# A new order of all steps in a hand-scheduled kernel: windowed attention, then one expert per sentence

## The chip, the cores and the metric

The kernel runs on one core of a Trainium2 chip. The metric is the time of one execution on the device, in microseconds (us). A core has five engines that run their own instruction streams and wait for each other by semaphores: TensorE (PE; loading its weights is shown apart as PEld), VectorE (DVE), ScalarE (ACT), GpSimd (POOL) and SyncE (SP). [...] Sixteen DMA engines move data between HBM and SBUF; here nearly all transfers are issued on POOL's queue.

## The reference

For 8 sentences of 576 positions, with 8 heads of width 64, the reference computes attention in which each position sees itself and the 63 before it; the heads are put side by side to x, 576 x 512. The mean of x over the sentence picks one of 8 experts, and the whole sentence goes through that expert:

```python
scores = scale * np.matmul(q, k.transpose(0, 1, 3, 2))
mask = (rel >= 0) & (rel < window)            # window = 64
attn = softmax(np.where(mask, scores, -1e9))
x = np.matmul(attn, v)                        # heads joined: B, S, D = 8, 576, 512
...
logits = x.mean(axis=1) @ w_gate              # D x 8
e = argmax(logits); gate = softmax(logits)[e]
out[b] = gate * (relu(x[b] @ w1[e]) @ w2[e])  # w1: 512 x 1024, w2: 1024 x 512 per expert
```

Inputs and output are fp32; q, k, v and the weights are cast to 16 bits on their way in.

## The kernel before, in words

A *unit* is one piece of the attention: for each of the 8 sentences (batches, b) four units of two heads each, over the first 512 positions, and a fifth, the *tail*, with the last 64 positions of all heads. Units are numbered 0 to 39; 5b + i is unit i of batch b, and i = 4 is the tail. An expert of a batch is worked off in 18 *chunks*: c b.0 to c b.7 multiply x by an eighth of w1 each (line 457, 8 matmuls of 512 columns), c b.8 does the same for the tail (line 466, 64 small matmuls), c b.9 to c b.16 are half-sums of four groups of output rows (line 499), and c b.17 is the output's tail (line 508).

The program has no loops that set its order. A long string, OPS, lists every step by a letter and a number, and the kernel issues the steps in exactly that order, each on its engine's queue (lines 532 to 559). A step that is early in the list but on another engine runs beside the others; what orders two engines are the data and buffers alone. The letters:

- T: transposes of one unit's q and k by PE into PSUM (lines 226, 233); U: copy of the q part out of PSUM (243, 247); k: copy of the k part into kT (253, 256). Where U and k of one unit are on different engines they read the same PSUM tile, and the second waits for the first.
- S: scores by PE (276), with b also a matmul that adds the mask (270); E: exp by ScalarE (289, or 292 in two halves after an S with m); K: mask by a multiply on VectorE (298), for units without b.
- l: row sums by PE (310, 315); n and R: ln and exp(-ln) on ScalarE, the reciprocal (352, 358); A: attention times V by PE (332, 340); X: A's result times R, into x and its sum for the mean (VectorE, 365, 371).
- g, G, H, I: the gate of a batch: products and a sum on VectorE with a small PE matmul (380 to 388), the largest logit and its index (399 to 403), softmax sum on ScalarE (428), reciprocal (434). P reads the expert's number into a register of POOL (409); everything behind P on POOL's queue waits for it.
- Q, t, L, W: loads on POOL's queue: q and k of a batch (Q 2b and 2b+1, line 110), their tails (133), five V tiles (L 5b to 5b+4, lines 141 and 145), four weight halves of the chosen expert (W 4b to 4b+3, lines 419 and 422: w1's columns for chunks 0 to 3 and 4 to 7, w2's rows for the first and the second half-sums). V: two copies that shift V (150, 151). Y and C: loads on SP's queue and casts for a part of batch 0.
- c: the next chunk of the list of chunks. r: the evacuation of the next finished chunk from PSUM: relu and gate (442, 444) or a copy of output rows (478, 483). O and o: store of the next finished output rows, by POOL's queue or by SP's (488). r b.j and O b.j below name the chunk they belong to.
- i, x, y, m, M, z: constants: the identity, two bands, the masks, zeroes.

A letter a or d behind T, U, k, A, C or r picks ScalarE or VectorE for a copy; m takes the PSUM buffer from the pool `mo`, three banks that chunks use too, instead of the step's own single buffer. So a step that takes a `mo` buffer waits until the third buffer before it has been read out.

The chunk list is fixed; where a chunk stands between the other steps is set by the place of the c in OPS. Batch b's first chunk needs x of all its five units, the gate and W 4b. The list holds 885 steps.

Of the kernel before, what the change touches and what calls it, by code (L numbers as in the profile page):

```python
# [1 line left out]
OPS = (  # L2
# [35 lines left out]
).split()  # L38

# [17 lines left out]
def kernel(  # L57
# [11 lines left out]
    B, H, S, D = q.shape  # L69
# [88 lines left out]
    mb = const.tile([128, 4, 16], FP16)  # L158
# [215 lines left out]
                    accum_out=pool[b][:, 1, n:n + 1])  # L374

    gpss = {}

    def gate0(b):
        gpr = gpool.tile([128, 2, NP, E], FP32, tag="gpr", name="gpr")
        nc.vector.tensor_tensor(  # L380
            out=gpr, in0=pool[b].unsqueeze(3).broadcast_to([128, 2, NP, E]),
            in1=wg.unsqueeze(1).broadcast_to([128, 2, NP, E]), op=ALU.mult)
        grd = gpool.tile([128, E], FP32, tag="grd", name="grd")
        nc.vector.tensor_reduce(out=grd, in_=gpr.rearrange("p c n e -> p e (c n)"), op=ALU.add,
                                axis=mybir.AxisListType.X)
        gps = ps_a.tile([128, E], FP32, tag="lb", name="gps")
        for c in range(2):
            nc.tensor.matmul(out=gps[64 * c:64 * c + 64], lhsT=ones32[:, 0:64], rhs=grd,
                             start=True, stop=True, skip_group_check=True)
        gpss[b] = gps  # L390
# [122 lines left out]
    def chunks():  # L513
        for b in range(B):
            for ft in range(9):
                yield lambda b=b, ft=ft: w1_chunk(b, ft)
            for r in range(4):
# [6 lines left out]

    unit_ops = {"K": unit_k, "E": unit_e, "l": unit_l, "n": unit_n, "R": unit_r, "X": unit_x}
    unit_eops = {"T": unit_tp, "U": unit_q, "k": unit_kt, "S": unit_s, "A": unit_a}
    batch_ops = {"g": gate0, "G": gate1, "H": gate_w, "I": gate2, "V": shift_v,
                 "P": pick, "W": load_w, "L": load_v, "t": load_tail}
    setup_ops = {"i": make_ident, "x": lambda: band(mb, 1), "y": lambda: band(mt, 0),
                 "m": main_mask, "M": tail_mask, "z": zero_v}  # L530

    with tc.manual_schedule():
        for op in OPS:
            c, x = op[0], op[1:].lstrip("abdm")
# [55 lines left out]
```

## Time and profile before

| what | us |
|---|---|
| median of 3 runs | 206.81 (206.77 to 208.1) |
| the profiled execution, its own time | 206.57 |
| span of its instructions in the profile | 205.0 |
| PE busy | 185.3 |
| ScalarE (ACT) busy | 133.6 |
| VectorE (DVE) busy | 119.5 |
| POOL busy, mostly issuing transfers | 110.0 |

The profile covers one execution. Its rows are read as follows. A timeline row has the start in us from the span's first instruction, the duration, the engine, the line, the operation, output <- inputs, and in square brackets the engine's idle time just before it and what ended that. A group row has the instructions of one kind with their count, then busy us and mean ns of one, then idle us before them. A row of the stage view has for each engine its busy us in that stretch and the number of instructions, then the granted PE clock as a share of full speed, the DMA share and GB/s. In the page's rows of digits each digit is a fortieth of the span, in tenths. Matmul ends are modelled, so a pipelined matmul looks longer than the pace at which matmuls follow each other. A transfer's row is its issue alone; the row "DMA to landing" tells the time from there to its arrival.

### The profile page before, as it was taken

What the parts mean: (1) busy time and instruction counts of PE and PEld (TensorE: products, weight loads), DVE (VectorE), ACT (ScalarE), POOL (GpSimd) and SP (SyncE); (2) the same over time, 40 slices, a digit from 0 to 9 for tenths busy, and PEclk for the clock granted to TensorE, in tenths of its full rate; (3) what the DMA queues carried; (4) which work ended last, traced back from release to release, by engine and by line L of the source; (5) the groups of instructions that cost most, each with busy time, mean ns of one, the idle gap of its engine ahead of it and who ended that gap; (6) DMA issues with size and microseconds to landing.
All of it is one profiled execution on the core that took longest, in us unless ns stands there. A gap on an engine that the chain in (4) does not pass through costs nothing.

```text
span 205.0 us, 8089 instructions
## 1 busy us (share of the span) xinstructions
PE 185.3 (90%) x3513; PEld 123.7 (60%) x3518; DVE 119.5 (58%) x343; ACT 133.6 (65%) x252; POOL 110.0 (54%) x157
## 2 busy tenths in 40 slices
PE   0549785999999999899999999999999999999991
PEld 0436563866685755657666676777566565655651
DVE  2055967786458695688588749566566258211041
ACT  3169998955588757879975992795577634525600
POOL 7968927514943384438824633436935622852650
PEclk9996999699999999999999999999999999999998
DMA  6999999999999999999999999999999999799995
GB/s 137 174 184 154 186 164 199 206 203 123 149 194 195 188 182 193 186 197 159 183 195 194 201 202 188 191 298 183 167 245 210 198 163 332 198 201 176 404 339 189
DMA packets 83538, 41.16 MB, mean 201 GB/s; under 512 B 48080, under 2 KB 80976, under 8 KB 83504
## 3 DMA queue, kind: packets, MB, share of 16 engines
q0 software_dynamic: 81696, 38.94, 137.0%
q1 hardware_dynamic: 1200, 1.64, 2.3%
q8 instruction: 27, 0.44, 0.8%
q10 hardware_dynamic: 608, 0.08, 0.3%
q14 instruction: 7, 0.06, 0.1%
HBM read 61.88 MB, written 9.44 MB: 348 GB/s over the span
## 4 chain that ended last, share of the span: by engine, by line
PE 74%; ACT 10%; DVE 8%; issue 3%; DMA 3%; POOL 0%; DVEq 0%; POOLq 0%
PE po L499 26%; PE ph L457 24%; PE tp L226 5%; PE ph L466 4%; PE s L276 4%; PE av L332 3%; DMA km<-in_k_dram 3%; PE po L508 3%; ACT pe L289 2%; PE lb L310 2%; ACT ln L352 2%; DVE kT L253 2%; ACT rl L358 2%; ACT pe L292 1%; DVE qt L243 1%
## 5 line engine op out<-in xcount | busy, mean ns | idle before, releaser
L457 PE MATMUL ph<-xm,w1b 128*64 128x512 f16 x512 | 60.8, 379 | 0.4 <-ACT kT L253 0.4
L499 PE MATMUL po<-w2b,hm 128*64 128x512 f16 x512 | 59.7, 379 | 0.0
L499 PEld LDWEIGHTS <-hm 128*64 128x64 f16 x512 | 29.1, 110 | 21.1
L457 PEld LDWEIGHTS <-w1b 128*64 128x64 f16 x512 | 30.1, 110 | 19.3 <-issue 0.7
L141 POOL DMA_DIRECT2D vw<-in_v_dram x32 | 28.9, 909 | 19.2 <-DMA w1b<-in_moe_w_dram 4.4
L442 ACT ACTIVATE hm<-ph,gw 128x512 f16<-128x512 f32 x40 | 27.5, 691 | 13.6 <-PE ph L457 13.3
L365 DVE CUSTOM_DVE_ANT_0 xm<-av,rl 128x512 f16<-128x512 f32 x32 | 21.8, 687 | 13.0 <-PE av L332 9.8
L352 ACT ACTIVATE ln<-lb 128x512 f32<-128x512 f32 (+1 forms) x40 | 22.6, 565 | 8.9 <-PE lb L310 7.3
L358 ACT ACTIVATE rl<-ln 128x512 f32<-128x512 f32 (+1 forms) x40 | 23.2, 593 | 3.6 <-DVE pool L365 3.4
L478 DVE COPY ob<-po 128x512 f32<-128x512 f32 x16 | 11.1, 691 | 24.8 <-PE po L499 24.8
L488 POOL DMA_DIRECT2D out_dram<-ob x28 | 15.5, 560 | 14.9 <-DMA w2b<-in_moe_w_dram 7.6
L444 DVE TENSOR_SCALAR hm<-ph,gw 128x512 f16<-128x512 f32 x24 | 18.0, 748 | 7.9 <-PE ph L457 7.6
L289 ACT ACTIVATE pe<-s 128x1024 f16<-128x1024 f32 x19 | 19.7, 1038 | 1.3 <-PE av L332 0.9
L298 DVE TENSOR_TENSOR pe<-pe,mask 128x1024 f16<-128x1024 f16 x26 | 17.7, 685 | 4.7 <-ACT pe L289 3.9
L226 PE MATMUL tp<-ident,qm 128*64 128x128 bf16 x256 | 14.6, 241 | 6.5 <-ACT qm L128 4.7
L276 PEld LDWEIGHTS <-kT 64*128 64x128 bf16 x576 | 10.8, 97 | 11.5 <-issue 7.7
L478 ACT COPY ob<-po 128x512 f32<-128x512 f32 x16 | 9.4, 590 | 12.1 <-PE po L499 12.1
L253 ACT COPY kT<-tp 128x512 bf16<-128x512 bf16 x16 | 9.5, 608 | 10.7 <-DVE qt L243 5.8
L226 PEld LDWEIGHTS <-qm 128*64 128x64 bf16 x256 | 10.9, 123 | 9.2 <-ACT qm L128 4.7
L422 POOL DMA_DIRECT2D w2b<-in_moe_w_dram x16 | 12.7, 798 | 6.9 <-DMA w1b<-in_moe_w_dram 2.1
L276 PE MATMUL s<-qt,kT 64*128 64x64 bf16 x512 | 12.7, 195 | 3.9 <-ACT kT L253 2.5
L419 POOL DMA_DIRECT2D w1b<-in_moe_w_dram x16 | 12.6, 792 | 6.6 <-PE ph L457 3.3
(82 smaller groups left out, 274.2 us busy)
## 6 DMA issues: line engine op xcount, KB each, us to landing
w1b<-in_moe_w_dram POOLq DMA_DIRECT2D x16, 512.0 KB, 8.5
w2b<-in_moe_w_dram POOLq DMA_DIRECT2D x16, 512.0 KB, 12.8
out_dram<-ob POOLq DMA_DIRECT2D x28, 256.0 KB, 8.6
vw<-in_v_dram POOLq DMA_DIRECT2D x32, 128.0 KB, 9.2
qm<-in_q_dram POOLq DMA_DIRECT2D x7, 512.0 KB, 9.9
km<-in_k_dram POOLq DMA_DIRECT2D x7, 512.0 KB, 9.4
out_dram<-ob SPq DMA_DIRECT2D x4, 256.0 KB, 3.9
out_dram<-obt POOLq DMA_DIRECT2D x14, 64.0 KB, 5.4
```

The lines of the kernel that those rows point to most:

```text
L141: nc.gpsimd.dma_start(out=vt[:, 2 * J + 1], in_=v[b, :, 128 * J:128 * J + 128].rearrange("h c d -> c h d"))
L226: nc.tensor.transpose(tp[p0:p0 + 64, n, r], t[:, 2 * i + hh, ts(r, 64)], ident)
L276: nc.tensor.matmul(out=sp[hh][:, ts(m, 64)], lhsT=kq, rhs=qt[p0:p0 + 64, m], start=not pm, stop=True, skip_group_check=True)
L289: nc.scalar.activation(out=po, in_=sp[0], func=AF.Exp, scale=scale)
L352: nc.scalar.activation(out=ln, in_=lb[:, 0:n], func=AF.Ln)
L358: nc.scalar.activation(out=rl, in_=lns.pop((b, i)), func=AF.Exp, scale=-1.0)
L365: nc.vector.tensor_tensor_reduce(out=xm[:, i], in0=av.rearrange("q r p -> q (r p)"), in1=rl, scale=1.0, scalar=0.0, op0=ALU.mult, op1=ALU.add,
L442: nc.scalar.activation(out=o, in_=i, func=AF.Relu, scale=g)
L444: nc.vector.tensor_scalar(out=o, in0=i, scalar1=g, scalar2=0.0, op0=ALU.mult, op1=ALU.max)
L457: nc.tensor.matmul(out=ph[64 * c:64 * c + 64], lhsT=w1t[:, kb, ts(2 * ft + c, 64)], rhs=xm[:, kb], start=(kb == 0), stop=(kb == 3), skip_g ...
L478: copy(e)(out=ob, in_=po)
L499: nc.tensor.matmul(out=po[64 * c:64 * c + 64], lhsT=hm[:, fb, ts(2 * r + c, 64)], rhs=w2t[:, fb], start=(fb == 0), stop=(fb == 7), skip_gr ...
```

## The change

The list OPS is replaced by another order of the same work, 891 steps. It was searched on a replay of the program in which two copies out of one PSUM tile take turns, and in which lengths are scattered in six cases. In it

- some copies and casts are on another engine: 9 instead of 13 q copies and 20 instead of 21 k copies on ScalarE, both casts of batch 0 on VectorE;
- nine instead of seven units are masked by a matmul (b), so 31 instead of 33 by a multiply; 16 instead of 14 value units and 16 instead of 15 score units use `mo` buffers;
- 38 instead of 35 stores go by POOL's queue, 2 instead of 5 by SP's; of the last batch's, O7.10, O7.14 and O7.16 go by POOL's, o7.12 and o7.17 by SP's;
- the gate's small PE matmul is a step of its own, j, somewhere behind g.

The first and the last lines of both lists and the code:

```diff
--- before
+++ after
@@ -1,40 +1,40 @@
 OPS = (
-    "Y0.24 Y1.24 Q0.48 Q1.48 i Ca0.24 Cd1.24 T1 Tm3 x ka3 Q0.2 Q1.2 Tm2 Tm0 Ud3 Ua1 mb Sb3 "
-    "ka1 kd2 z Ua2 E3 Ua0 Q2 ka0 Q3 Sm2 S0 l3 E2 t0 E0 n3 Smb1 E1 Tm5 T4 K0 y L2 kd5 Tm8 L3 "
-    "ka4 Tm7 Mb Ua4 l1 K2 ka8 Sb4 R3 L4 Ud5 T6 n1 l2 kd7 Ud8 E4 L1 R1 Sb5 n2 l4 L0 Ud6 t1 ka6 "
-    "n4 R4 V0 Am3 l0 A1 L7 E5 Ud7 n0 T9 X3 Am2 kd9 R2 X1 Sb7 X2 R0 Q4 E7 A0 Q5 Ud9 l5 L5 Am4 "
-    "Smb6 X4 n5 Sb8 L6 E6 X0 L8 R5 l7 Sm9 T12 n7 E9 g0 Tm10 Ud12 G0 Ud10 E8 L9 Tm11 ka12 ka11 "
-    "S12 Tm13 H0 l6 Ud11 R7 V1 ka10 n6 kd13 t2 A5 Q6 X5 T14 E12 Ud13 A7 K9 Q7 X7 P0 l8 kd14 "
-    "W0 Am6 R6 S10 n8 l9 W1 Ud14 K12 E10 A8 Sm14 n9 S11 E14 X6 E11 Tm15 l12 Tm17 T16 K14 R8 "
-    "K10 Ud17 X8 Ud15 Tm18 n12 kd17 S13 W3 I0 A9 l10 ka15 K11 Ud18 c W2 ka18 t3 n10 c c R9 "
-    "l14 L11 rd E13 X9 c S17 L10 rd ra L13 n14 g1 G1 rd P1 c ra c R14 rd c c c ra L14 K13 ra "
-    "c c c H1 Ua16 ra l11 R12 c rd L12 W5 ra n11 c ka16 c l13 c ra V2 W4 Q9 A12 Q8 I1 c X12 "
-    "Am14 A10 R10 c rd X14 rd E17 T19 n13 S15 R11 X10 K17 ka19 Sm18 E18 c R13 Am11 l17 c Ud19 "
...
-    "ra l38 V7 c n38 ra R36 c c c ra W27 c O E39 O K39 c rd A35 O c X35 c l39 Am36 A38 rd R38 "
-    "I6 X36 ra c n39 O c rd Am39 O R39 O ra l37 c X38 X39 c rd A37 c c rd n37 c R37 ra X37 g7 "
-    "rd c ra ra G7 H7 c rd c O O O O P7 W28 c c ra W29 c ra W30 W31 O O O O O O O O O O O c c "
-    "ra O c rd O I7 c c c ra O c ra O c rd ra c c c ra ra ra c c c ra ra c ra c c ra c c rd o "
-    "rd o c c c c rd o rd o c ra o "
+    "Y0.24 Q0.48 Q1.48 Q0.2 x Cd0.24 y i Q1.2 Y1.24 Q3 Cd1.24 z Tm3 Tm2 mb T0 Tm1 ka3 ka2 ka0 "
+    "t0 Ud3 Ud2 Q2 Sb3 L0 L3 ka1 L1 L2 E3 Smb2 L4 Ud0 l3 Ud1 t1 S0 T4 E2 kd4 Ud4 n3 Smb1 E0 "
+    "Mb K0 E1 R3 Q4 L9 Tm5 Sb4 Tm7 Tm8 Ud5 Q5 ka5 kd8 E4 L5 kd7 l1 n1 T6 l4 n4 Ud7 l2 Sb5 ka6 "
+    "n2 R1 R4 l0 V0 A3 Ud6 L7 Am1 n0 E5 T9 X3 Am2 Ud9 S7 R2 L8 E7 Ud8 X1 R0 l5 X2 L6 n5 Smb6 "
+    "A0 Am4 K7 ka9 E6 t2 X4 X0 Sb8 l7 g0 n7 T12 j0 Q6 Sm9 Tm10 G0 Ud12 kd12 E8 Ud10 H0 E9 "
+    "Tm13 Tm11 R7 K9 l6 R5 ka10 Sb12 Ud11 ka13 V1 n6 Q7 l8 P0 Ud13 W0 I0 kd11 T14 Am5 A7 X7 "
+    "A6 Ud14 kd14 L12 n8 X5 E12 R6 l12 n12 Sm14 X6 S11 l9 E14 Smb10 Tm17 E11 n9 T18 W1 Ud17 "
+    "A9 W2 E10 S13 kd18 Ud18 L13 Tm15 Ud15 l10 Am8 R8 W3 kd15 ka17 T16 K14 L11 c X8 L14 n10 "
+    "E13 R9 c ra X9 c R10 c rd c g1 K11 rd S17 j1 G1 ra ra c H1 L10 c rd l14 K13 c t3 ra c P1 "
+    "n14 Q8 ra c c rd c V2 Ua16 c c ra ka16 l11 A10 X10 Am12 W4 c Q9 R12 X12 n11 ra W5 R11 "
+    "A11 rd W6 T19 E17 c l13 n13 R13 Ua19 I1 X11 c Sm18 S15 K17 L15 rd E18 W7 R14 A13 c l17 "
+    "ra X13 A14 c L16 L17 X14 g2 n17 Tm20 E15 ra kd19 c Ud20 ra L18 kd20 T22 S19 Sm16 E19 L19 "
...
+    "Ud38 A33 ra ka38 Am34 l35 T39 X33 c n35 W22 c ra X34 A31 X31 g6 kd39 c O Sm38 R35 O S37 "
+    "ra E38 j6 c c G6 P6 Ud39 E37 ra ra c V7 K38 rd H6 c l36 c K37 W24 n36 S39 A35 l37 ra rd "
+    "E39 c ra n37 c X35 R36 c A37 c ra l38 Am36 K39 ra c c O R37 rd X37 n38 Am39 X36 O c rd c "
+    "I6 l39 W27 R38 c n39 O O A38 rd R39 c W25 W26 ra X39 X38 g7 c j7 O c G7 c ra c P7 rd ra "
+    "c c O W29 O c ra c O rd H7 O ra c O c W28 W31 ra O ra O c ra c c ra rd c c c c rd c W30 "
+    "I7 O ra O c rd c c ra rd O c O O rd c O rd O O c rd c c O ra c c rd c O rd ra rd c c O "
+    "rd O c c ra O O c c c c ra rd o O c ra O c ra o "
 ).split()
@@ -374,6 +374,7 @@
                     accum_out=pool[b][:, 1, n:n + 1])
 
     gpss = {}
+    grds = {}
 
     def gate0(b):
         gpr = gpool.tile([128, 2, NP, E], FP32, tag="gpr", name="gpr")
@@ -383,6 +384,10 @@
         grd = gpool.tile([128, E], FP32, tag="grd", name="grd")
         nc.vector.tensor_reduce(out=grd, in_=gpr.rearrange("p c n e -> p e (c n)"), op=ALU.add,
                                 axis=mybir.AxisListType.X)
+        grds[b] = grd
+
+    def gate_mm(b):
+        grd = grds.pop(b)
         gps = ps_a.tile([128, E], FP32, tag="lb", name="gps")
         for c in range(2):
             nc.tensor.matmul(out=gps[64 * c:64 * c + 64], lhsT=ones32[:, 0:64], rhs=grd,
@@ -524,7 +529,7 @@
 
     unit_ops = {"K": unit_k, "E": unit_e, "l": unit_l, "n": unit_n, "R": unit_r, "X": unit_x}
     unit_eops = {"T": unit_tp, "U": unit_q, "k": unit_kt, "S": unit_s, "A": unit_a}
-    batch_ops = {"g": gate0, "G": gate1, "H": gate_w, "I": gate2, "V": shift_v,
+    batch_ops = {"g": gate0, "j": gate_mm, "G": gate1, "H": gate_w, "I": gate2, "V": shift_v,
                  "P": pick, "W": load_w, "L": load_v, "t": load_tail}
     setup_ops = {"i": make_ident, "x": lambda: band(mb, 1), "y": lambda: band(mt, 0),
                  "m": main_mask, "M": tail_mask, "z": zero_v}
```

35 rows, old and new, of the table OPS are left out of this document.

## The prediction

> **What bounds the kernel now.** I read the page first, then busy time by stage, then the chain of waits, then the row-by-row timeline where the stages meet.
>
> ```profile
> span 205.0 us, 8089 instructions
> PE 185.3 (90%) x3513; PEld 123.7 (60%) x3518; DVE 119.5 (58%) x343; ACT 133.6 (65%) x252; POOL 110.0 (54%) x157
> PE   0549785999999999899999999999999999999991
> PEclk9996999699999999999999999999999999999998
> DMA  6999999999999999999999999999999999799995
> ```
>
> PE has holes in the first eight slices and hardly any later. The DMA engines are full from the second slice on. The stage view says the same in us; its cuts are the start of the first expert chunk c0.0 (42.70), c2.0, c3.0 and the last matmul.
>
> ```profile
> core 0: us, PE busy (x) PEld busy (x) DVE busy (x) ACT busy (x) POOL busy (x), PEclk, DMA share, GB/s
> 12.40:42.70 30.30, 23.54 (x613) 17.71 (x617) 21.37 (x65) 27.51 (x52) 19.28 (x24) 0.89 1.72 184
> 42.70:83.60 40.90, 40.70 (x770) 27.90 (x771) 26.91 (x76) 28.87 (x56) 21.05 (x26) 1.00 1.56 178
> 83.60:107.50 23.90, 23.02 (x482) 15.22 (x478) 18.35 (x55) 20.14 (x38) 12.95 (x17) 1.00 1.62 183
> 107.50:200.80 93.30, 93.22 (x1598) 59.38 (x1592) 49.29 (x138) 53.20 (x102) 45.80 (x71) 1.00 1.26 228
> ```
>
> Before 42.70 ScalarE (ACT) is the busiest: 27.5 of 30.3 us. From 42.70 PE works without a break. What must PE still do there? The chain gives the pace when nothing waits:
>
> ```profile
> 112.59 0.34 PE s L276 x16
> ...
> 131.23 0.45 PE tp L226 x16
> ...
> 167.29 0.51 PE av L332 x32
> ...
> 185.06 6.91 PE ph L457 x64
> 191.96 1.01 PE ph L466 x64
> 192.97 6.91 PE po L499 x64
> 199.88 0.89 PE po L508 x16
> ```
>
> The last four rows are one batch's expert: 15.7 us, eight times 125.8. After c0.0 stand also 21 units' transposes (16 at 0.45, five tails at half: 8.3), 25 score units (7.5, at 0.34 and tails less), 28 row sums (two 512-column matmuls each, as the quarter of a chunk 0.22, tails half: 5.5), 30 value units (0.25, tails half: 6.8) and seven gates' tiny matmuls (taken as 1.0). Together 154.9. It ran from 42.70 to 200.8, 158.1: only 3.2 are lost after c0.0. So the time is: start of c0.0, plus 154.9 of PE work, plus a few us of stalls, plus 4.2 from the last matmul to the end of the span, plus 1.57 between the span (205.0) and the execution's own 206.57. The runs shown have a median of 206.81, 0.24 above it.
>
> **The change, step by step.** Counting the steps of both lists on each side of c0.0: PE's work behind c0.0 is the same set of steps, only reordered, so 154.9 stays. What can move is c0.0, the stalls and the tail.
>
> (1) *When ScalarE is ready for c0.0.* c0.0 waited here:
>
> ```profile
> 41.61 0.42 DVE L243 COPY qt<-tp 128x512 bf16<-128x512 bf16 x1
> 42.06 0.59 ACT L253 COPY kT<-tp 128x512 bf16<-128x512 bf16 x1 [1.09 <-DVE qt L243]
> 42.70 1.27 PE L457 MATMUL ph<-xm,w1b 128*64 128x512 f16 x10 [0.38 <-ACT kT L253]
> ```
>
> The middle row is ka15. It reads the tile that Ud15 has just read (copies out of one tile take turns); c0.0 takes ka15's PSUM buffer. ScalarE's work from the first exp (13.16) to there groups as follows:
>
> ```profile
> L289 ACT ACTIVATE pe<-s 128x1024 f16<-128x1024 f32 x8 | 8.3, 1041 | 1.1 <-PE av L332 0.7 <-PE s L276 0.4
> L253 ACT COPY kT<-tp 128x512 bf16<-128x512 bf16 x7 | 4.2, 632 | 1.3 <-DVE qt L243 1.1 <-PE tp L226 0.2
> L292 ACT ACTIVATE pe<-s 128x512 f16<-128x512 f32 x6 | 3.4, 629 | 0.0
> L243 ACT COPY qt<-tp 128x512 bf16<-128x512 bf16 x1 | 0.6, 580 | 0.0
> L247 ACT COPY qtt<-tpt 128x256 bf16<-128x256 bf16 x1 | 0.4, 378 | 0.0
> ```
>
> The new list has the same exp, ln and reciprocal steps there, but 5 kT copies for 7 (-1.26), no qt and no qtt copy (-0.96), and E10 in two halves (2 x 0.63 - 1.04 = +0.22): -2.0, and about 0.3 back because neighbouring rows overlap by 0.1: -1.7. The 1.09 before ka15 goes too: the buffer of c0.0 is now Tm17's, freed by ka17, whose partner Ud17 stands five steps ahead of the last VectorE step before c0.0. So ScalarE could be through at 42.65 - 1.7 - 1.1 = 39.9. The first exp starts as before: four transposes back to back now end at 11.8, where the mask made Sb3 start before. VectorE takes over four qt copies, a cast and a kT copy (about 2.7 us) and gives up three mask multiplies and X8 (2.8): even, and it was busy 21.4 of 30.3. PE makes two more masks by matmul (about 0.43 each, 0.9): hidden in its 6.8 idle us; without that cover +0.9.
>
> (2) *When the loads are there.* Q7 (K of batch 3) and W0 (first weight half):
>
> ```profile
> L110 POOL DMA_DIRECT2D km<-in_k_dram x1: 881/881/881, 28.7 to 28.7; - x1
> DMA to landing us min/median/max: 9.0/9.0/9.0
> ...
> L419 POOL DMA_DIRECT2D w1b<-in_moe_w_dram x1: 752/752/752, 32.0 to 32.0; - x1
> DMA to landing us min/median/max: 8.3/8.3/8.3
> ```
>
> Q7 landed at 37.7, W0 at 40.3: one full queue, 2.6 us per 512 KB, emptied in order. Both lists put the same loads ahead of W0, so W0 stays at 40.3 even if the gate comes earlier. Behind Q7 PE has four transposes (1.8), a value unit's tail, a score unit, a row sum and a value unit (0.9) before c0.0: 37.7 + 2.7 = 40.4. So c0.0 lies between 40.4 and 43.6 (nothing won, and the masks uncovered). Before, the same 2.7 us of work took 5.0. I take 41.0, near the low end since ScalarE's 39.9 lies below it: **-1.7**.
>
> (3) *Weights behind it.* V tiles now stand between the weight halves: W1 lands one V tile later (0.64 by size), near 43.5, and c0.4 is due at 41.0 + 4 x 0.86 = 44.4. W3 lands two later, near 49.2; c0.10 is due near 50.4. Hidden, with about a microsecond to spare; c0.0 beyond that can't pull the rest along.
>
> (4) *P1 on POOL's queue.* P1 reads the expert number of batch 1, and all loads behind it wait:
>
> ```profile
> 48.63 0.69 POOL L145 DMA_DIRECT2D vw<-in_v_dram  x1 [6.75 <-DVE hm L444]
> ...
> 49.00:53.00 4.00, 4.00 (x95) 3.05 (x92) 1.35 (x2) 3.09 (x8) 3.89 (x6) 1.00 1.36 89
> 53.00:57.00 4.00, 4.00 (x42) 2.67 (x39) 2.31 (x4) 1.84 (x4) 3.92 (x5) 1.00 1.18 176
> ```
>
> POOL stood 6.75 us, the queue ran dry, and 4 us passed at 89 GB/s instead of 176: 2 us of loads lost. The new list has two more V loads ahead of P1 (11.3 us of queue behind W0 for 10.3, by size) and G1 about a microsecond earlier, so this hole should close. PE did not wait for it, so I book 0 and keep 2 us of margin: loads then come early enough for a PE that is 1.7 us early.
>
> (5) *Stalls behind c0.0.* c2.0 to c3.0 took 23.9 for 22.4 of work, the largest loss, 1.5, with ScalarE at 84%. The new list spreads ScalarE's copies (in that stage 20.2 us by mean durations instead of 24.4) but gives VectorE 21.4 instead of 19.2. The gates' matmuls (new step j) no longer stand right behind their sums. From -1.5 to +3; I take **-0.4**.
>
> (6) *Tail.* Output O7.16 goes by POOL's queue, o7.17 by SP's as before:
>
> ```profile
> L488 POOL DMA_DIRECT2D out_dram<-ob x2: 540/540/540, 195.4 to 195.9; - x2
> DMA to landing us min/median/max: 4.5/4.6/4.6
> ...
> L488 SPq DMA_DIRECT2D out_dram<-ob x1: 332/332/332, 200.6 to 200.6; - x1
> DMA to landing us min/median/max: 2.7/2.7/2.7
> ```
>
> POOL's queue was still full there; the new list stores more before, and O7.16 is ready 0.9 us ahead of o7.17. Between 0 and +1; I take **+0.2**.
>
> Sum: 206.57 - 1.7 - 0.4 + 0.2 = **204.7**.
>
> **The rivals.**
> *A: c0.0 does not come early.* The clock row has two slices at 6: PE at half clock. A transpose unit then takes twice as long:
>
> ```profile
> 38.81 0.64 PE L226 MATMUL tp<-ident,qm 128*64 128x128 bf16 x8
> ...
> 39.67 0.50 PE L310 MATMUL lb<-pe,ones 128*64 128x512 f16 x2
> 40.00 0.39 PE L226 MATMUL tp<-ident,qm 128*64 128x128 bf16 x8
> ...
> 40.45 0.39 PE L226 MATMUL tp<-ident,qm 128*64 128x128 bf16 x8
> ```
>
> From 38.81 to 39.67 is one unit, 0.86; from 40.00 to 40.45 the next, 0.45. In the new list the 2.7 us behind Q7 set c0.0; at half clock throughout they take 5.4, c0.0 comes at 43.1, and the time is 206.6 + 0.4 - 0.2 = 206.8. For it: in the page each halved slice follows one in which PE was only 4 or 5 tenths busy, and PE will have holes before Q7 again. Against it: from about 40 on the clock was full. [...]
>
> *B: slower.* An engine falls behind PE in the middle. By mean durations ScalarE has 0.95, 0.91 and 0.92 of PE's time between c1.0, c2.0, c3.0 and c4.0, VectorE 0.97 in the second. If each of these three stages loses the 1.5 us of the worst stage of before, in waits for PSUM buffers, and the rest loses its 1.7, that is 6.2 for 3.2, +3; with c0.0 halfway (-0.8) and a full tail (+1), 209.8. From 1.5 us of stalls more than before, the main case's gain is gone. Against it: in the worst stage ScalarE's figure was 1.09.
>
> *C: more than expected.* c0.0 at 40.4, all of the 1.5 us gone, no tail: 206.57 - 2.3 - 1.5 = 202.8. For it: P1's hole closes. Against it: every hand-off must fit.
>
> **How the numbers follow.** Main case 0.45, itself 203.7 to 205.7; A 0.2; B 0.2; C 0.15. About 1% (2.1 us) is what a measurement of this kernel can tell from no change, so faster means below 204.7: C and a good half of the main case, 0.42. Slower means above 208.9: three quarters of B, 0.15. Within: 0.43. The range 202.6 to 208.9 leaves out that part of B and a third of C, 0.2 in all.
>
> **What would show it.** Right: c0.0 starts near 41.0, PE has nearly no idle time behind it, no 89 GB/s stretch near 50, and POOL's wait at P1 is covered. Wrong: c0.0 after 42, with ka17 or Q7 named (step 1 or 2); PE waits for W1 or W3 in batch 0 (3); idle PE between 60 and 125 behind VectorE or ScalarE (5); over 4.5 us from last matmul to end (6).

## The result, and the profile after

| | before | after |
|---|---|---|
| median of 20 runs each, us | 207.66 (206.56 to 209.9) | 205.5 (204.76 to 208.15) |
| ratio of the times, 95% interval | | 0.9932 (0.9905 to 0.996) |
| the profiled execution, its own time, us | 206.57 | 204.83 |
| span, us | 205.0 | 203.2 |

The change makes the kernel 0.7% faster; the interval reaches from 0.4% to 0.95%. The ratios here and below leave out runs more than 1.5% above the fastest of the same kernel. The profiled pair differs by 1.74; both lie at the fast end of their kernel's runs. The page of after, the rows that answer to those of before:

```profile
span 203.2 us, 8111 instructions
...
PE 184.5 (91%) x3522; PEld 124.4 (61%) x3522; DVE 120.1 (59%) x347; ACT 132.0 (65%) x247; POOL 112.4 (55%) x160
...
PE   0496786799999999999999999999999999999991
...
PEclk9999999999999999999999999999999999999997
```

PE still has its holes in the first eight slices, but in this execution none of them is followed by half clock, which before had two slices of (16 to 19 and 36 to 40 us). The clock row does not show the beginning: in the first 11 us the transposes of both kernels follow each other at half pace, a group of 8 every 0.43 us instead of 0.22. The stage view of after, cut at c0.0, c2.0, c3.0 and the last matmul (PE, PEld, DVE, ACT, POOL busy, then clock, DMA share, GB/s):

```profile
12.40:42.15 29.75, 23.23 (x622) 16.13 (x623) 20.70 (x61) 25.79 (x49) 18.94 (x24) 1.00 1.76 179
42.15:82.76 40.61, 40.61 (x792) 26.70 (x788) 26.29 (x76) 30.23 (x59) 21.75 (x27) 1.00 1.57 192
82.76:105.45 22.69, 22.69 (x470) 15.28 (x464) 19.20 (x57) 17.85 (x34) 14.14 (x18) 1.00 1.69 186
105.45:198.95 93.50, 93.42 (x1596) 62.79 (x1592) 49.33 (x136) 54.15 (x102) 46.10 (x72) 1.00 1.25 230
```

Two things are to be seen. Behind c0.0 PE waits for next to nothing, and the worst stage of before (c2.0 to c3.0, 23.90) takes 22.69. And c0.0 is hardly earlier, 42.15 for 42.70, although ScalarE's work ahead of it fell from 27.51 to 25.79. Where did that go? Rows of PE tell it (start, duration; in brackets the idle time before and what ended it):

```profile
17.80 0.41 PE L226 MATMUL tp<-ident,qm 128*64 128x128 bf16 x8 [1.55 <-DMA qm<-in_q_dram]
...
41.92 0.39 PE L226 MATMUL tp<-ident,km 128*64 128x128 bf16 x8
42.15 0.38 PE L462 MATMUL ph<-xm,w1b 128*64 128x512 f16 x2
```

c0.0 (line 462 here; the lines behind the new step j are five further down) waits for nothing itself. But ahead of 17.80 PE stands 1.55 us until Q2, the q of batch 1, has landed, and begins Tm5 0.05 behind it; before, Q2 and Q3 had landed by 15.76 and PE came to Tm5 at 17.29. The chain of waits, followed back from c0.0, runs through PE, ScalarE and VectorE to Tm5, from there to Q2 without another load, and on through POOL's issues to steps that POOL computes itself. Pieces of it, in order of time:

```profile
5.35 0.47 POOL ident L178
5.82 1.58 POOL km L110 x2
...
8.74 9.02 DMA qm<-in_q_dram
17.80 0.64 PE tp L226 x16
```

The loads are late from the start of the queue on. The view of busy time in 5 us windows, first after, then before:

```profile
5.00:10.00 5.00, 2.18 (x38) 1.94 (x40) 1.99 (x8) 0.59 (x2) 5.00 (x8) 1.00 1.25 152
10.00:15.00 5.00, 4.83 (x88) 2.96 (x86) 1.46 (x4) 3.55 (x6) 4.12 (x6) 1.00 1.41 149
```

```profile
5.00:10.00 5.00, 2.82 (x48) 2.14 (x46) 0.28 (x1) 0.53 (x2) 4.93 (x8) 1.00 1.37 173
10.00:15.00 5.00, 2.44 (x55) 1.69 (x52) 2.97 (x8) 3.46 (x7) 3.39 (x5) 1.00 1.55 186
```

The queue moved 152 and 149 GB/s instead of 173 and 186. The timeline of POOL in after shows what it did instead:

```profile
3.89 0.28 POOL L183 TENSOR_SCALAR_AFFINE_SELECT mb<-mb 128x64 f16<-128x64 f16 x1
...
5.31 0.51 POOL L178 TENSOR_SCALAR_AFFINE_SELECT ident<-ident 128x128 bf16<-128x128 bf16 x1
5.77 1.63 POOL L110 DMA_DIRECT2D km<-in_k_dram  x2
...
8.74 0.93 POOL L110 DMA_DIRECT2D qm<-in_q_dram  x1
```

From 3.89 to 5.8 POOL itself computes the two bands and the identity (x, y, i, five steps). Only then does it issue Q1.2 and Q3, in the row of 5.77, and Q2 comes at 8.74 where before issued it at 5.44.

### The profile page after: what moved, and what is told of

Same layout as the page of the kernel before. It is cut to its first block, busy times and chain, and to the rows that moved or that the text cites. A ratio compares the mean times of both kernels' runs of the same rounds, so it can differ in the third digit from the quotient of the medians.

```text
span 203.2 us, 8111 instructions
## 1 busy us (share of the span) xinstructions
PE 184.5 (91%) x3522; PEld 124.4 (61%) x3522; DVE 120.1 (59%) x347; ACT 132.0 (65%) x247; POOL 112.4 (55%) x160
## 4 chain that ended last, share of the span: by engine, by line
PE 66%; DMA 13%; POOL 6%; issue 6%; ACT 4%; DVE 2%; POOLq 1%; ACTq 0%; DVEq 0%
PE ph L462 21%; PE po L504 20%; PE tp L226 6%; DMA w2b<-in_moe_w_dram 4%; DMA w1b<-in_moe_w_dram 4%; DMA qm<-in_q_dram 4%; PE s L276 4%; PE av L332 3%; PE lb L310 3%; PE ph L471 3%; POOL out_dram L493 3%; PE po L513 2%; ACT ln L352 2%; POOL km L110 1%; ACT pe L289 1%
## 5 line engine op out<-in xcount | busy, mean ns | idle before, releaser
L462 PEld LDWEIGHTS <-w1b 128*64 128x64 f16 x512 | 31.8, 110 | 18.7 <-issue 0.4
L504 PEld LDWEIGHTS <-hm 128*64 128x64 f16 x512 | 30.1, 110 | 19.3
L447 ACT ACTIVATE hm<-ph,gw 128x512 f16<-128x512 f32 x39 | 26.6, 694 | 13.5 <-PE ph L462 13.3
L493 POOL DMA_DIRECT2D out_dram<-ob x31 | 17.2, 557 | 24.7 <-DMA w1b<-in_moe_w_dram 7.5
L483 ACT COPY ob<-po 128x512 f32<-128x512 f32 x18 | 10.6, 587 | 23.5 <-PE po L504 20.7
L449 DVE TENSOR_SCALAR hm<-ph,gw 128x512 f16<-128x512 f32 x25 | 18.7, 749 | 12.1 <-PE ph L462 11.6
L298 DVE TENSOR_TENSOR pe<-pe,mask 128x1024 f16<-128x1024 f16 x24 | 16.3, 686 | 4.0 <-ACT pe L289 3.3
L253 ACT COPY kT<-tp 128x512 bf16<-128x512 bf16 x19 | 11.2, 594 | 9.8 <-PE tp L226 8.1
L243 DVE COPY qt<-tp 128x512 bf16<-128x512 bf16 x25 | 10.4, 418 | 9.9 <-PE tp L226 4.8
L483 DVE COPY ob<-po 128x512 f32<-128x512 f32 x14 | 9.7, 691 | 10.7 <-PE po L504 10.5
L332 PEld LDWEIGHTS <-vw 128*64 128x64 f16 x512 | 12.4, 112 | 4.3 <-issue 1.2
```

The lines of the kernel that those rows point to most:

```text
L447: nc.scalar.activation(out=o, in_=i, func=AF.Relu, scale=g)
L449: nc.vector.tensor_scalar(out=o, in0=i, scalar1=g, scalar2=0.0, op0=ALU.mult, op1=ALU.max)
L462: nc.tensor.matmul(out=ph[64 * c:64 * c + 64], lhsT=w1t[:, kb, ts(2 * ft + c, 64)], rhs=xm[:, kb], start=(kb == 0), stop=(kb == 3), skip_g ...
L483: copy(e)(out=ob, in_=po)
L493: (nc.scalar if n and eng is nc.sync else eng).dma_start(out=dst, in_=src)
L504: nc.tensor.matmul(out=po[64 * c:64 * c + 64], lhsT=hm[:, fb, ts(2 * r + c, 64)], rhs=w2t[:, fb], start=(fb == 0), stop=(fb == 7), skip_gr ...
```

## The experiments

All times are against the kernel before on the same chip, whose median was 207.63 to 208.29 in these comparisons. "c0.0" and "last chunk" (c7.17) are the starts in the profiled execution.

| kernel | median us (runs) | ratio, 95% interval | Tm5 | c0.0 | last chunk |
|---|---|---|---|---|---|
| before | 207.66 (20) | 1 | 17.29 | 42.70 | 199.72 |
| after | 205.5 (20) | 0.9932 (0.9905 to 0.996) | 17.80 | 42.15 | 197.87 |
| loads first | 203.21 (6) | 0.9776 (0.9732 to 0.9819) | 15.50 | 39.85 | 196.12 |
| old head, new rest | 205.24 (6) | 0.9876 (0.9834 to 0.9919) | 17.39 | 43.02 | 198.57 |
| new head, old rest | 208.02 (12) | 1.0003 (0.9966 to 1.004) | 17.78 | 42.54 | 200.17 |
| old copies | 208.87 (12) | 1.0047 (1.0012 to 1.0081) | 17.31 | 44.89 | 200.45 |
| before, loads first | 208.38 (12) | 1.0003 (0.9966 to 1.0041) | 16.43 | 41.94 | 199.62 |
| second band later | 203.52 (6) | 0.9779 (0.9738 to 0.982) | 15.89 | 40.24 | 196.41 |
| Q2 ahead of t0 | 204.09 (4) | 0.981 (0.9762 to 0.9859) | 15.62 | 41.29 | 196.82 |
| P1 early | 208.19 (12) | 0.9998 (0.996 to 1.0037) | 19.17 | 45.01 | 203.19 |
| after, early matmuls | 206.99 (9) | 0.9941 (0.9902 to 0.9981) | 18.94 | 45.72 | 201.63 |
| loads first, early matmuls | 204.78 (4) | 0.9855 (0.9821 to 0.9889) | 16.09 | 41.95 | 198.12 |
| before, one relu earlier | 206.94 (10) | 0.9968 (0.9936 to 1.0) | 17.37 | 42.04 | 199.42 |

**Loads first.** The theory: c0.0 of after is set by loads that POOL issues behind its own steps. One line is reordered:

```diff
-    Q0.2 x Cd0.24 y i Q1.2 Y1.24 Q3 Cd1.24 z Tm3
+    Q0.2 i Q1.2 Cd0.24 Y1.24 Q3 x y Cd1.24 z Tm3
```

> The changed kernel with only POOL's first steps reordered: the loads Q0.2, Q1.2 and Q3 are issued ahead of the two bands (x, y), only the identity (i) stays ahead of Q1.2. Theory (loads set the head): in the changed kernel POOL computed bands and identity from 3.9 to 5.8 us while the load queue ran half empty (149 to 152 GB/s from 5 to 15 us, where the kernel before had 173 to 186), so Q2 landed at 17.75 and W0 at 41.4. Then here Q2 lands near 16.7, W0 near 40.4, c0.0 starts near 41.3 instead of 42.15 and the span is near 202.4 instead of 203.2. Rival (hand-offs between ScalarE, VectorE and PE set the head): loads land earlier, c0.0 stays within 0.3 us of 42.15, and the span stays at 203.2.

c0.0 came 2.30 us earlier, at 39.85, and the time fell by 2.3 below after's, more than expected. POOL, the windows and PE of this kernel:

```profile
3.89 0.31 POOL L178 TENSOR_SCALAR_AFFINE_SELECT ident<-ident 128x128 bf16<-128x128 bf16 x1
4.13 1.61 POOL L110 DMA_DIRECT2D km<-in_k_dram  x2
...
8.27 0.91 POOL L110 DMA_DIRECT2D qm<-in_q_dram  x1
```

```profile
5.00:10.00 5.00, 2.80 (x50) 2.56 (x52) 2.34 (x9) 1.17 (x2) 4.86 (x9) 1.00 1.40 181
10.00:15.00 5.00, 4.76 (x100) 2.71 (x96) 1.92 (x6) 4.03 (x7) 4.73 (x7) 1.00 1.63 184
```

```profile
15.50 0.41 PE L226 MATMUL tp<-ident,qm 128*64 128x128 bf16 x8 [0.32 <-DMA qm<-in_q_dram]
...
39.85 0.60 PE L462 MATMUL ph<-xm,w1b 128*64 128x512 f16 x4
```

Q1.2 and Q3 are issued 1.64 us earlier, the queue fills to 181 GB/s at once, and Q2 lands 2.30 us earlier though it is issued only 0.47 earlier: it had been waiting behind the others. Not all of the 2.30 is the reordering: the very first load of the queue, issued at 1.46 in both, landed at 7.07 in after and at 6.37 here. But in the five executions with after's first steps Q2 landed at 17.27 to 19.13, in the three with the loads first and Q2 in this place at 15.45 to 16.04. From Tm5 to c0.0 it is 24.35 us in both kernels (42.15 - 17.80 and 39.85 - 15.50). That it is the same to the hundredth is in part chance: here the chain passes through one more load, a V tile that landed at 30.47. This version beats both kernels; with the next but one, whose ratio is the same within the noise, it is the best of this study.

**Before, loads first.** The same in the kernel before (Q0.2 and Q1.2 ahead of i):

```diff
-    Y0.24 Y1.24 Q0.48 Q1.48 i Ca0.24 Cd1.24 T1 Tm3 x ka3 Q0.2 Q1.2 Tm2
+    Y0.24 Y1.24 Q0.48 Q1.48 Q0.2 Q1.2 i Ca0.24 Cd1.24 T1 Tm3 x ka3 Tm2
```

> The kernel before, with its loads Q0.2 and Q1.2 ahead of the identity on POOL's queue, nothing else moved. The theory that ScalarE and not the loads set c0.0 in the kernel before: the loads come up to 0.9 us earlier, c0.0 stays within 0.3 of 42.70, the time within 0.4 of the kernel before. The rival, that loads bound both kernels: c0.0 comes 0.5 to 0.9 earlier and the time falls as much.

By the time nothing is won (1.0003). In the profile c0.0 lies 0.76 earlier, outside the 0.3; but the half clock that before has at 36 to 40 us is absent here. The kernel with one relu earlier (below), whose head is before's, comes to 42.04 in an execution whose clock stays full from 18.2 us on, with Tm5 at 17.37. So 0.66 of before's 42.70 comes and goes with the execution. Against that one Tm5 is 0.94 earlier here and c0.0 only 0.10; as the clock differs between these executions too (half from 16.2 to 19.7 here), the profiles do not separate the two causes. What stays is the time: earlier loads help the new head and not, within 0.4%, the old one.

**Second band later.** Loads first, and y behind L4:

```diff
-    Y1.24 Q3 x y Cd1.24 z ... Q2 Sb3 L0 L3 ka1 L1 L2 E3 Smb2 L4 Ud0
+    Y1.24 Q3 x Cd1.24 z ... Q2 Sb3 L0 L3 ka1 L1 L2 E3 Smb2 L4 y Ud0
```

> The kernel after with its first loads ahead of POOL's own steps, as in the run with loads first, and in addition the second band (y, two steps of POOL, 0.55 us together) put behind L4. The loads theory: Q2 and all loads behind it come about 0.5 us earlier, c0.0 starts at 39.4 where loads first had 39.85, and the time falls by another 0.3 to 0.5, to about 202.8. The rival, that with loads first ScalarE or PE sets c0.0 again: c0.0 stays within 0.2 of 39.85 and the time within 0.2 of 203.2.

The theory missed here: Q2 was issued 0.47 earlier, and landed 0.4 later. The whole queue was that much later, from loads on that the edit does not touch: Q1.2, issued at 4.15 here and at 4.13 with loads first, landed at 9.55 and 9.14.

```profile
7.80 0.91 POOL L110 DMA_DIRECT2D qm<-in_q_dram  x1
```

```profile
L110 POOL DMA_DIRECT2D qm<-in_q_dram x1: 909/909/909, 7.8 to 7.8; - x1
...
DMA to landing us min/median/max: 8.0/8.0/8.0
```

That is a landing at 15.85 (the 8.0 is rounded); in the kernel with loads first it was 15.45. Here the full queue (179 and 184 GB/s from 5 to 15 us) landed Q2 when the transfers ahead of it were through, though it was issued earlier. Tm5 to c0.0 is 24.35 once more (40.24 - 15.89). So putting POOL's steps behind the loads paid until the queue was full, and in this one further try not beyond.

**Q2 ahead of t0.** Loads first, Q2 ahead of the tail loads, and T4, which needs them, behind Tm5:

```diff
-    ka0 t0 Ud3 Ud2 Q2 Sb3 ... S0 T4 E2 kd4 Ud4 n3 ... L9 Tm5 Sb4
+    ka0 Ud3 Ud2 Q2 t0 Sb3 ... S0 E2 n3 ... L9 Tm5 T4 kd4 Ud4 Sb4
```

> The kernel with loads first, and in it the load Q2 ahead of the two tail loads t0 on POOL's queue; the transposes T4 of the tail, which need t0, and their two copies stand behind Tm5 instead of ahead of it. The theory that c0.0 comes 24.35 us after Tm5 begins, and Tm5 begins when Q2 has landed: Q2 lands at 14.2 to 14.5 instead of 15.45, Tm5 starts at about 14.9, when PE comes to it, c0.0 at 39.2 to 39.4 instead of 39.85, and the time falls by 0.3 to 0.6 below 203.2. The rival, that with loads first the copies and exps behind Tm5 set the pace by themselves: c0.0 stays within 0.2 of 39.85 or later and the time within 0.3 of 203.2 or above.

The rival came. Q2 was issued 1.3 us earlier (6.96), landed only 0.25 earlier (15.20), and c0.0 came 1.44 later: the tail's transposes had filled PE's wait for Q2, and behind it their copies hold up the next unit.

```profile
15.62 0.41 PE L226 MATMUL tp<-ident,qm 128*64 128x128 bf16 x8
...
17.84 0.29 PE L276 MATMUL s<-qtt,kT 64*128 64x64 bf16 x8 [0.74 <-DVE qtt L247]
```

Here it is 25.67 from Tm5 to c0.0: the 24.35 belongs to one order of the copies, not to the work alone. With that order it was 24.35 in three executions, 24.76 in a fourth (new head, old rest), and 25.8 to 26.8 in the three that had half clock on the way (P1 early and the two with early matmuls).

**Old copies.** After, with 14 copies ahead of c0.0 on the engine that they have in the kernel before:

```diff
-    ka2 Ud2 Ud0 Ud1 kd4 Ud4 ka5 kd8 ka9 kd12 ka13 kd11 kd15 ka17
+    kd2 Ua2 Ua0 Ua1 ka4 Ua4 kd5 ka8 kd9 ka12 kd13 ka11 ka15 kd17
```

> The changed kernel with the 14 copies of the head (U and k ahead of c0.0) that changed their engine put back on the engine they had before; the order stays. ScalarE then has about 2 us more of copies ahead of c0.0. Theory of the prediction (ScalarE's work sets the head): c0.0 1 to 2 us later, 43.2 to 44.2. Rival (loads set the head): c0.0 within 0.4 us of 42.15 and the span within 0.5 of 203.2.

c0.0 came 2.74 later than in after, at 44.89, though W0 had landed by 40.3. ScalarE again bounds the end of the head, as it did before the change, and with the same kind of row: a copy that waits for its partner out of the same tile.

```profile
44.25 0.58 ACT L253 COPY kT<-tp 128x512 bf16<-128x512 bf16 x1 [0.54 <-DVE qt L243]
...
44.89 0.62 PE L462 MATMUL ph<-xm,w1b 128*64 128x512 f16 x4 [0.22 <-ACT kT L253]
```

So the new places of the copies are worth 2 to 3 us at c0.0 (part of the 2.74 may be half clock: 0.95 on the mean in this stage), and after could cash them in only as far as its loads let it.

**Old head, new rest; new head, old rest.** One list up to c0.0 and the other from there on, with the few steps that one has ahead of c0.0 and the other behind it put at the joint:

```diff
 old head: ... K11 Ud18 | L12 W2 kd18 L13 L11 | c and the list of after behind its first c
 new head: ... K14 L11 | X8 K11 | c and the list of before behind its first c
```

> The order of the kernel before up to c0.0, then the new order (L11, L12, L13, W2 and one copy, which the new order has ahead of c0.0, stand directly ahead of it). Theory (most of the gain is in the stalls behind c0.0): c0.0 near 42.7 as before, then 155.7 us to the last chunk as in the changed kernel, span near 203.8, so about 0.6 above the changed kernel and 1.2 below before. Rival (the gain hangs on the new head, whose loads and copies are further on): span 204.6 or more.

> The new order up to c0.0, then the order of the kernel before (X8 and K11 first). Theory (head 0.55, rest 1.3): c0.0 near 42.15, then 157.1 us as before, span near 204.5, so 0.5 below before. Rival (the head makes the gain): span near 203.4.

From c0.0 to the last chunk it is 157.0 in before and 157.6 with the old rest, 155.7 in after and 155.6 with the new rest. The new rest alone gives the whole gain of the change (0.9876; that it gives more is not shown, the interval overlaps that of after). The new head alone gives nothing (1.0003) where 0.5 us was expected: its c0.0 was at 42.54.

**P1 early.** After, with P1 (which takes the expert's number, and holds everything behind it on POOL's queue) right behind G1:

```diff
-    X8 L14 n10 E13 ... j1 G1 ra ra c H1 L10 c rd l14 K13 c t3 ra c P1 n14 Q8
+    X8 n10 E13 ... j1 G1 P1 L14 L10 t3 ra ra c H1 c rd l14 K13 c ra c n14 Q8
```

> The kernel after, with P1 put right behind G1 on POOL's queue, ahead of L14, L10 and t3, as it stands in the kernel before. The theory that the hole near 50 us is closed by the loads put ahead of P1: the stretch 49 to 53 us falls from 168 GB/s to about 100, Q9 lands 1 to 2 us later, and PE waits for it at Tm20, whose slack is below 1 us: the time rises by 0.5 to 1.5. The rival, that these loads would have been early enough anyway: c0.0 to the last chunk stays within 0.3 of 155.7 and the time within 0.3 of the kernel after.

The ratio rose from after's 0.9932 to 0.9998, some 1.4 us, the upper end of what was expected; Q9 landed later than expected, at 67.34 instead of 61.59 (2.9 later when counted from c0.0). The windows of after first, then of this kernel, then its POOL and its PE:

```profile
49.00:53.00 4.00, 4.00 (x96) 2.61 (x92) 1.25 (x3) 2.41 (x5) 2.84 (x4) 1.00 2.08 168
53.00:57.00 4.00, 4.00 (x84) 2.55 (x82) 2.55 (x5) 2.72 (x6) 3.62 (x6) 1.00 1.34 204
```

```profile
49.00:53.00 4.00, 4.00 (x78) 2.35 (x76) 2.30 (x7) 2.56 (x7) 1.43 (x2) 1.00 0.81 80
53.00:57.00 4.00, 4.00 (x82) 2.49 (x78) 1.90 (x3) 2.43 (x5) 4.00 (x6) 1.00 1.47 96
```

```profile
51.42 0.69 POOL L145 DMA_DIRECT2D vw<-in_v_dram  x1 [11.44 <-DVE gnm L408]
```

```profile
64.69 1.05 PE L462 MATMUL ph<-xm,w1b 128*64 128x512 f16 x8 [0.39 <-DMA w1b<-in_moe_w_dram]
...
67.38 0.41 PE L226 MATMUL tp<-ident,km 128*64 128x128 bf16 x8 [1.42 <-DMA km<-in_k_dram]
```

POOL stands 11.44 us at P1 and the queue runs dry (80 GB/s from 49 to 53 us where after has 168); 13 to 16 us later PE waits 0.39 for W4 and 1.42 for Q9. From c0.0 to the last chunk it is 158.2 instead of 155.7. This execution, at 210.19, is one of the two longest of the twelve. Its head was late (Q2 landed at 19.13, issued 0.09 later than in after), which has nothing to do with P1 and is left out of the 2.5; behind c0.0 its clock was full.

**Early matmuls.** Twelve 512-column matmuls on zeros ahead of the first transposes, which do not touch the result, put into after and then into the kernel with loads first:

```diff
-    Cd1.24 z Tm3
+    Cd1.24 z F12 Tm3
```

> The kernel after, with twelve extra 512-column matmuls on zeros ahead of the first transposes, so that PE has work from about 4 us on; the result is not touched. The loads theory (in the kernel after, c0.0 waits for loads that POOL issues late): the granted clock is full from some 5 us earlier than in the kernel after, and c0.0 starts within 0.3 of its 42.15 all the same, the time within 0.5 of 205. The clock theory (rival A: half clock on PE's steps ahead of c0.0 decides): c0.0 starts at 41.6 or earlier and the time falls by 0.6 or more. [...]

> The kernel with loads first, and the twelve extra matmuls on zeros ahead of its first transposes. The theory that early work on PE itself brings half clock into the steps up to 22 us: the clock row again shows slices of 7 or less among the first five, c0.0 starts after 40.3 instead of 39.85, and the time is 0.5 to 1.5 above 203.2. The rival, that the run with the extra matmuls alone was late because its loads came late by chance: the clock is full from 10 us on, c0.0 lies within 0.3 of 39.85 and the time within 0.4 of 203.2.

By the medians both were slower, by 1.5 and 1.6 us; by the ratios the first is not to be told from after (0.9941 and 0.9932), the second clearly slower (0.9855 and 0.9776). In the profile of the first, c0.0 came at 45.72, which neither theory had: Q2 landed at 18.9 by itself (from the same issue time), and the clock was at half from 8.2 to 11.6 and from 18.5 to 25.3 us. So it decides nothing about c0.0; that is why the second was made. Its PE:

```profile
2.64 3.81 PE L550 MATMUL wps<-warm 128*128 128x512 bf16 x9
...
13.52 0.41 PE L276 MATMUL s<-qt,kT 64*128 64x64 bf16 x16
16.09 0.47 PE L226 MATMUL tp<-ident,qm 128*64 128x128 bf16 x8 [2.17 <-DMA qm<-in_q_dram]
```

```profile
13.90:16.10 2.20, 0.04 (x4) 0.01 (x2) 1.00 (x2) 1.77 (x4) 0.94 (x2) 1.00 2.02 164
16.10:19.50 3.40, 3.40 (x60) 2.73 (x62) 0.42 (x1) 1.08 (x2) 3.02 (x4) 0.53 2.37 156
```

The transposes from 6.4 us on ran at full clock (0.24 us apart where after's first ones are 0.43), so PE was through its work sooner, and then stood 2.17 us instead of 0.32 for the same load. The clock fell to 0.53 for the next 3.4 us, just where PE has a backlog. c0.0 came 2.1 later, 0.6 of it by Q2.

**Before, one relu earlier.** To see what the stalls behind c0.0 are made of, one step of before moved: the relu of c2.0 ahead of Ud24, a copy that waits its turn.

```diff
-    R16 E23 ka24 Ud24 rd l20 X19 ra K23 Sm22
+    R16 E23 ka24 rd Ud24 l20 X19 ra K23 Sm22
```

> The kernel before with one step moved: VectorE's relu of chunk c2.0 (rd) ahead of Ud24, the copy that waits its turn behind ScalarE's copy out of the same tile; in the kernel before, VectorE stands idle 0.95 us for that copy, the relu comes at 85.63, and PE waits 0.59 us for it in Sm22. The theory that the stalls behind c0.0 come from copies that stand waiting for their turn with other work queued behind them: the wait in Sm22 goes, c2.0 to c3.0 takes 23.2 to 23.4 instead of 23.9, and the time falls by about 0.5. The rival, that a stall taken away is paid at the next hand-off: the wait at T28 grows as much, c2.0 to c3.0 stays within 0.2 of 23.9 and the time does not move.

In that stage it came as the theory said. VectorE's rows, then PE's:

```profile
84.14 0.75 DVE L444 TENSOR_SCALAR hm<-ph,gw 128x512 f16<-128x512 f32 x1 [0.19 <-PE ph L457]
84.89 0.29 DVE L247 COPY qtt<-tpt 128x256 bf16<-128x256 bf16 x1
```

```profile
85.11 0.41 PE L276 MATMUL s<-qt,kT 64*128 64x64 bf16 x16
...
87.61 0.41 PE L226 MATMUL tp<-ident,qm 128*64 128x128 bf16 x8 [0.29 <-DVE kT L253]
```

The relu runs while ScalarE copies, Sm22 waits no more, the wait at T28 stays 0.29, and c2.0 to c3.0 takes 106.16 - 83.06 = 23.10. That the whole kernel gains by it is not shown. The median fell by 0.8, but the interval of the ratio reaches 1. And in this execution the next two stages took 0.24 and 0.76 longer than in before, 0.55 of it one stop of PE with nothing that ended it. From c0.0 to the last chunk it was 157.38, where this order unmoved took 157.02, 157.63 and 157.68 (before; new head, old rest; before, loads first).

## Why the prediction was right or wrong

The forecast for the profiled execution, 204.7, is 0.13 off its 204.83, but by luck: its terms are wrong and their errors cancel. And by the ratio of all runs the gain is 0.7% where the forecast stood for 1%. In the span the 1.7 us fall into c0.0 -0.55, c0.0 to the last chunk -1.30, the last chunk to the end +0.1. I had -1.7, -0.4 and +0.2. Even the -0.55 may be the execution's: the head of before came to 42.04 in the one with a relu moved behind it.

- *Step 1, ScalarE, was right*: 27.51 - 25.79 = 1.72 less of work, as worked out, the wait of ka15 gone, and the old copies cost 2.7 when put back. With the loads first ScalarE was through with ka17 at 39.09, where I had 39.9. "The first exp starts as before" also held (13.20).
- *Step 2 failed.* It set the floor of c0.0, 40.4, by Q7 and W0 at the end of the head, and put a delay of earlier loads at nothing. "Both lists put the same loads ahead of W0, so W0 stays at 40.3": it landed at 41.4, as these rows of after say (the first of the two loads is W0, 31.3 + 10.1).

```profile
L424 POOL DMA_DIRECT2D w1b<-in_moe_w_dram x2: 752/795/838, 31.3 to 33.0; - x2
...
DMA to landing us min/median/max: 10.1/11.0/11.9
```

c0.0 did not wait for it, though: it came 0.74 later, at the end of the chain that began with Q2, Tm5 plus 24.35. I had counted the loads on POOL's queue and not the other instructions on it; x, y and i stood ahead of Q1.2 and Q3, and Q2 waited behind those. With the loads first Q2 landed 2.3 earlier, and c0.0 came at 39.85, below my floor. Why W0 was late is another matter and stays open: Q7, ahead of it, landed at 37.95, only 0.2 later than before, and 3.46 us from Q7 to W0, where all the other kernels have 2.5 to 2.8, are seen in this execution alone.
- *Step 3 was right*: W1 landed at 44.84 for c0.4 at 45.60, W3 at 50.85 for c0.10 at 51.62, 0.8 us to spare each.
- *Step 4 was right* that the hole closes: 168 GB/s for 89. That its place matters in this list, the run with P1 early shows: 1.4 us by the ratio, 2.5 behind c0.0 in its profile.
- *Step 5 was mis-sized*: -1.3 for -0.4. Its worst stage gave back 1.2 alone (23.90 to 22.69). The two joints show that it is the order behind c0.0 that does it, and the moved relu shows one such stall, 0.59 us, with its cause: a copy waiting its turn, and on the same queue behind it a step that PE needs. That every other stall has this cause was not tested, and the time of the whole kernel did not clearly follow.
- *Step 6*: +0.1 for +0.2.

Of the rivals, A's outcome, c0.0 not early, is what came, but not by its mechanism: the clock of the profiled execution was full from 13.3 us on. That half clock ahead of c0.0 goes with a later c0.0 is seen with the early matmuls (loads first: 0.53 for 3.4 us, c0.0 2.1 later, 0.6 of it by Q2), and of the 20 runs of after the eight with a mean clock below 0.99 have spans of 204.5 to 206.6, while eleven of the twelve others have 203.1 to 203.9. No run of the three kernels with loads first and without extra matmuls, 16 in all, has a mean clock below 0.99. In 69 runs of the kernel before, those below 0.99 are not longer than the others (median spans 205.8 and 206.3). The one trace of such a long execution with after's head, that of P1 early, shows a late load first and half clock behind it (last section); for the eight runs themselves it stays open. B did not come: no wait of PE behind c0.0 is over 0.25. C's time, 202.8, is nearly reached by the kernel with loads first (203.09 in the profiled execution).

## What to carry to other kernels

Where an engine issues loads, look whether its own computing steps delay them: here 1.9 us of such steps on POOL stood ahead of loads, and with the loads first Q2 landed and c0.0 started 2.30 us earlier (0.7 of it is seen in the very first load already), with the queue at 181 instead of 152 GB/s from 5 to 10 us. Going further won nothing here (second band later: c0.0 at 40.24 for 39.85). When a bound is taken away, look for the wait at the beginning of its chain (here 1.55 us for Q2), not only at the end. Where two engines copy out of one tile, look whether one stands in line for its turn (here VectorE, 0.95 us at Ud24) with a step behind it that a third engine needs; moving that step took away the stall of 0.59 us here, if not clearly any time.

## What was unexpected of the hardware

- With 1.9 us of computing on POOL, early, a load issued 0.47 us later landed 2.3 us later (0.7 of it is seen in the very first load already), and 10 us of the queue ran at 150 instead of 182 GB/s. Each of these loads also takes 0.7 to 0.9 us of POOL at its issue. Whether POOL's computing slows the queue by anything but late issues, no run here shows.
- Early matmuls brought PE to full clock sooner, and the kernel with loads first was slower with them (0.9855 for 0.9776): 2.17 us of waiting at full clock were followed by 3.4 us at 0.53, while in after 1.55 us of waiting at the same place were followed by full clock. Before had half clock from 16.01 to 19.43 and from 36.49 to 39.91; in the 3.41 us ahead of each, PE was busy for 1.47 and 1.68. In after, cut into pieces of 3.41 us from 13.28 on, PE was busy for 2.27 or more in each piece up to 197.61, and the clock was full in all of them. What sets the clock, no run here shows. P1 early has after's head, but there Q2 landed 1.38 later. Below are its stretch with the wait for Q2 and the one behind it, then the stretch with that wait in after, which was followed by full clock:

```profile
15.97:19.39 3.42, 0.89 (x26) 0.51 (x26) 1.43 (x5) 2.01 (x4) 0.48 (x1) 1.00 2.17 166
19.39:22.80 3.41, 3.41 (x60) 2.71 (x56) 0.42 (x1) 1.08 (x2) 3.37 (x5) 0.50 1.88 142
```

```profile
16.70:20.11 3.41, 2.31 (x64) 1.86 (x66) 1.16 (x3) 2.51 (x5) 1.90 (x3) 1.00 2.37 158
```

In P1 early Tm5 began 1.37 later than in after and c0.0 came 2.86 later: as much again was lost behind the late load.
- PE stopped within a run of equal instructions, with nothing that ended the wait. In after this, 0.51 us, stood on the way to c0.0:

```profile
39.26 0.22 PE L226 MATMUL tp<-ident,km 128*64 128x128 bf16 x1
39.98 0.38 PE L226 MATMUL tp<-ident,km 128*64 128x128 bf16 x7 [0.51 <-issue]
```

It is no accident of this execution: at the same instruction PE stopped for 0.24 us with loads first, 0.23 with the second band later and 0.51 in new head, old rest. What it is, no run here shows.
